# Channel attention and gated FFN on one core: the first batch's G/H tiles in other slots and PSUM banks, a bf16 epsilon product, and sums of squares folded before the norm products

## The chip, the core and the metric

The kernel runs on one core of a Trainium2 chip. The metric is the device time of one execution in microseconds (us). Five runs of the kernel before gave a median of 808.2 us (808.1 to 808.29).

## The reference

For each of 4 batches, q, k and v are 6016 x 256 matrices. Every column of q and k is divided by its norm over the 6016 rows; the 256 x 256 scores between k's and q's columns go through a softmax along the last axis; v times this matrix is the attention output. All rows then pass through a gated feed-forward layer of width 1536.

```python
B, N, C = (4, 6016, 256)
qn = q / (np.linalg.norm(q, axis=1, keepdims=True) + 1e-06)
kn = k / (np.linalg.norm(k, axis=1, keepdims=True) + 1e-06)
s = kn.transpose(0, 2, 1) @ qn / tau
s = s - s.max(-1, keepdims=True)
a = np.exp(s)
a /= a.sum(-1, keepdims=True) + 1e-09
x = (v @ a).reshape(B * S, D)
gate = 1.0 / (1.0 + np.exp(-(x @ w_gate)))
val = x @ w_val
out = gate * val @ w_out
```

## The kernel before

**G and H.** The softmax matrix and the first layer's weights are multiplied once per batch: G = a @ w_gate and H = a @ w_val, each 256 x 1536, so that v goes directly into the gated layer. A tile of G or H (`gh`) is a pair of matmuls into a PSUM tile `ps_gh` (`gh_mms`), and an eviction that divides by the row sums (`gh_store`, on ScalarE where the piece's channel block is 0, else on VectorE). For the first batch the pieces come in the order of the weight loads (`gh_first`): columns 0 to 255 and 256 to 511 (half width), then two groups of 512; in each, G's two channel blocks and then H's two. So tiles 0 to 3 serve slots 0 and 1, tiles 4 to 7 slots 2 and 3, tiles 8 to 11 slots 4 to 7, tiles 12 to 15 slots 8 to 11.

**Chunks and slots.** A batch has 47 row tiles of 128, handled in 12 chunks of 4 (the last has 3). A chunk has 12 slots, one for each 128 columns of the hidden layer. In a slot `glu` issues two matmuls into `ps_gate` and two into `ps_val` (512 columns each, both with vT, the transposed rows of v, as the moving operand), tanh on ScalarE (`g_sb`), and one VectorE operation that gives `hT`. `ps_gate` and `ps_val` have two PSUM banks each (`psg`, `psv`). So a slot's `ps_val` waits for the `hT` of two slots before.

**The second layer.** `out_work` lists the products of the chunk before with w_out, some of them with sums of blocks of `hT` that VectorE makes (`a_sum`, tile `sums`) and sums of blocks of w_out. `run_work` issues a share of them in each slot, as `ps_o`. ScalarE copies the results out, GpSimd adds blocks (`m_sb`, `out_sb`), and SyncE stores.

**Side work.** `side_work(b)` puts the preparation of batch b + 1 into the slots of batch b, counted from the batch's start (slot 98 is slot 2 of chunk 8). Loads of q, k and v are issued by GpSimd. The transposes of v (`transpose_v`) are DMA transposes issued by SyncE, one chunk ahead; only the first chunk's vT is made on TensorE. Score products go into `ps_s`. Squares of q and k (ScalarE) are added up in `acc`, a bf16 tile of 128 x 4 x 256 per tensor (`acc_add`, VectorE). Then `norms_mm` sums `acc` over partitions: for each of q and k, 4 row tiles x 2 channel blocks, a weight load of 128 x 128 and a product with one column of ones. `root_seed` (VectorE) and `root_steps` (13 small GpSimd operations) take the square root, `norms_inv` the reciprocal, `spread_both` and `copy_rk` bring k's factors into a row layout, and `exps` gives the exponentials `e_sb`.

**Row sums.** `sums_start` opens the PSUM tile `ps_r` with the product of `ones_row` and `eps_row`, one row high, which puts epsilon into it; `row_sums` adds the products of `e_sb` with ones and takes the reciprocal. For the first batch there are two such tiles, made ahead of the chunks; later batches have one each (`all_sums`, slot 116).

**The first batch's start.** Squares, scores and norms of batch 0 run ahead of the first chunk, and so do tiles 0 to 3. The other tiles are in the first chunk: tile 4 between gate and val products of slot 0 (`between` of `glu`), the rest behind the slots that `gh_slots` lists, all of them in the two banks of `pso`. The order on every engine is the order in which the program issues (`manual_schedule`).

Of the kernel before, what the change touches and what calls it, by code (L numbers as in the profile page):

```python
# [9 lines left out]
FP32 = mybir.dt.float32  # L10
BF16 = mybir.dt.bfloat16
INT32 = mybir.dt.int32
ACT = mybir.ActivationFunctionType
ALU = mybir.AluOpType
# [39 lines left out]
def kernel(  # L54
# [20 lines left out]
    nc = tc.nc  # L75
    P = nc.NUM_PARTITIONS
# [8 lines left out]
    CB = C // P  # L85
# [3 lines left out]
    TPC = 4  # L89
# [12 lines left out]
    def pool(name, bufs, **kw):  # L102
        return ctx.enter_context(tc.tile_pool(name=name, bufs=bufs, **kw))

    consts = pool("consts", 1)
# [14 lines left out]
    pso = pool("pso", 2, space=PSUM)  # L120
    pss = pool("pss", 1, space=PSUM)
    psm = pool("psm", 1, space=PSUM)
# [3 lines left out]
    def mm(out, lhsT, rhs, start, stop, **kw):  # L126
        nc.tensor.matmul(out, lhsT=lhsT, rhs=rhs, start=start, stop=stop, **kw)  # L127
# [43 lines left out]
    one_two = consts.tile([P, 2], BF16)  # L171
    nc.vector.memset(one_two[:, 0:1], 1.0)
    nc.vector.memset(one_two[:, 1:2], 2.0)
    ones_row = consts.tile([1, P], FP32)
    nc.vector.memset(ones_row, 1.0)
    eps_row = consts.tile([1, CB, 2], FP32)
    nc.vector.memset(eps_row[:, :, 0:1], 1e-9)
    nc.vector.memset(eps_row[:, :, 1:2], 2e-9)
    shift = consts.tile([P, 1], FP32)
# [12 lines left out]
    for f0, nf in pieces:  # L192
        for w, src in enumerate((moe_w_gate, moe_w_val)):
            nc.gpsimd.dma_start(
                out=w_sb[w][f0 // FG][:, :, ds(f0 % FG, nf)],
# [7 lines left out]
    for n in range(FC // TPC):  # L203
        w_f32[n] = f32pool.tile([P, TPC, C], FP32, tag="f32", name="w_f32")
        nc.gpsimd.dma_start(
            out=w_f32[n], in_=moe_w_out.rearrange("(t p) c -> p t c", p=P)[:, n * TPC : (n + 1) * TPC, :]
# [16 lines left out]
    st = {}  # L223
# [29 lines left out]
    def norm_mms(ps, sqs, nt, first, last, order=(0, 1)):  # L253

        for w in order:
            sq = sqs[w]
            for u in range(nt):
                for j in range(CB):
                    mm(
                        ps[:, w * CB + j : w * CB + j + 1],  # L260
                        sq[:, u, ds(j * P, P)],
                        ones_bf[:, 0:1],
                        start=(first and w == order[0] and u == 0 and j == 0),
                        stop=(last and u == nt - 1),
                        skip_group_check=True,
                    )
# [12 lines left out]
    def acc_add(b, g, w):  # L279
# [5 lines left out]
            out=acc[:, :nt, :], in0=acc[:, :nt, :], in1=st[b]["sq", w][:, :nt, :], op=ALU.add  # L285
        )

    def norms_mm(b):
        s = st[b]
        s["n"] = psm.tile([P, 2 * CB], FP32, tag="m", name="ps_n")  # L290
        norm_mms(s["n"], s["acc"], TPC, True, True)

    def scale_x(b, j):
        s = st[b]
# [143 lines left out]
    gh_first = [(f0, nf, w, i) for f0, nf in pieces for w in range(2) for i in range(CB)]  # L438
# [15 lines left out]
    def gh_store(b, piece, ps, act):  # L454
        s = st[b]
        f0, nf, w, i = piece
        dst = s["gh"][w][f0 // FG][:, i, ds(f0 % FG, nf)]
        if act:
            nc.scalar.activation(out=dst, in_=ps[:, :nf], func=ACT.Copy, scale=s["rrow"][i][w])
        else:  # L460
            nc.vector.tensor_scalar(  # L461
                out=dst, in0=ps[:, :nf], scalar1=s["rrow"][i][w], scalar2=None, op0=ALU.mult
            )

    def gh(b, piece, pl, tag, act=None):
        gh_store(b, piece, gh_mms(b, piece, pl, tag), piece[3] == 0 if act is None else act)
# [25 lines left out]
    def glu(b, ci, f, between=None):  # L492
        t0, nt = groups[ci]
        n = nt * P
        G, H = st[b]["gh"]
        vT = vts[b, ci]
        if f == 0:
            hts[b, ci] = hpool.tile([P, FC, CH], BF16, tag="hT", name="hT")
        ps_gate = psg.tile([P, CH], FP32, tag="g", name="ps_gate")
        ps_val = psv.tile([P, CH], FP32, tag="v", name="ps_val")  # L500
        for ps, w in ((ps_gate, G), (ps_val, H)):
            for ib in range(CB):
                mm(
                    ps[:, :n],
                    w[f // (FG // P)][:, ib, ds(f % (FG // P) * P, P)],
                    vT[:, ib, :nt, :],
                    start=(ib == 0),
                    stop=(ib == CB - 1),
                )
            if between is not None and w is G:  # L510
                between()
        g_sb = gpool.tile([P, CH], FP32, tag="g", name="g_sb")
        nc.scalar.activation(out=g_sb[:, :n], in_=ps_gate[:, :n], func=ACT.Tanh, scale=0.5)  # L513
        nc.vector.scalar_tensor_tensor(  # L514
            out=hts[b, ci][:, f, :n],
            in0=g_sb[:, :n],
            scalar=1.0,
            in1=ps_val[:, :n],
            op0=ALU.add,
            op1=ALU.mult,  # L520
        )
# [123 lines left out]
    def store():  # L645
        while stores:
            b, ci = stores.pop(0)
            t0, nt = groups[ci]
            nc.sync.dma_start(out=out_rows[b][:, t0 : t0 + nt, :], in_=ffn.pop((b, ci))[:, :nt, :])
# [40 lines left out]
    acc = st[0]["acc"]  # L690
    last0 = len(groups0) - 1
    adds, ends = [], []
    for g, (t0, nt) in enumerate(groups0):
# [6 lines left out]
        while adds:  # L700
            w, last_sq = adds.pop()
# [42 lines left out]
    def side_work(b):  # L744


        side = {}

        def at(slot, fn, *a):
            side.setdefault(divmod(slot, FC), []).append((fn, a))  # L750

        for ci in range(NCH):
            nb, nci = (b, ci + 1) if ci + 1 < NCH else (b + 1, 0)
            lb, lci = (b, ci + 2) if ci + 2 < NCH else (b + 1, ci + 2 - NCH)
            if nb < B:
                at(ci * FC + 2, transpose_v, nb, nci)
            if lb < B:
                at(ci * FC + 0, load_v, lb, lci)
            if (b, ci) == (0, 0):
                for i in range(FC // TPC):  # L760
                    at(8, copy_w_out, i)
                for n, m in enumerate((1, 0, 3, 2, 4)):
                    for i in range(FC // TPC):
                        at(10 + 2 * n, sum_w_out, m, i)
        n = b + 1
        if n == B:
            return side
        first, last = (14 if b == 0 else 0), 8 * FC
        for g, (t0, nt) in enumerate(groups):
            s0 = first + g * (last - first) // NCH  # L770
            if b == 0:
                at(max(0, s0 - 12), load_qk, n, t0, nt)
            elif s0 >= 24:
                at(s0 - 24, load_qk, n, t0, nt)
            for u in range(nt):
                at(first + (t0 + u) * (last - first) // NT, score, n, t0, u)
            if g == 0:
                at(s0, acc_start, n)
            for i, (fn, w) in enumerate(((acc_square, 0), (acc_add, 0), (acc_square, 1), (acc_add, 1))):
                at(s0 + 1 + 2 * i, fn, n, g, w)  # L780
        if n + 1 < B:
            for g, (t0, nt) in enumerate(groups[:3]):
                at(NCH * FC - 24 + 8 * g, load_qk, n + 1, t0, nt)
        s0 = 8 * FC + 2
        at(s0, norms_mm, n)
        at(s0 + 1, root_seed, n)
        at(s0 + 1, root_steps, n)
        at(s0 + 10, norms_inv, n)
        at(s0 + 12, spread_both, n)
        at(s0 + 13, copy_rk, n)  # L790
        at(s0 + 14, scale_x, n, 0)
        at(s0 + 14, scale_x, n, 1)
        at(s0 + 15, exps, n, 0)
        at(s0 + 16, exps, n, 1)
        at(s0 + 18, all_sums, n)
        at(s0 + 18, gh_tiles, n)
        for i, piece in enumerate(gh_order):
            at(s0 + 19 + 9 * i // 4, gh, n, piece, *((pss, "s"), (psm, "m"))[i % 2])
        return side

    gh_slots = ((5, 6, 7), (8,), (9, 10), (11,), (12,), (13, 14), (15,))
    prev = None
    for b in range(B):
        side = side_work(b)
        for ci in range(NCH):
            final = (b, ci) == (B - 1, NCH - 1)
            for f in range(FC):
                first = (b, ci, f) == (0, 0, 0)  # L810
                glu(b, ci, f, (lambda: gh(0, gh_first[4], pso, "o")) if first else None)
                if prev is not None:
                    if f == 4:
                        store()
                    if f + final in NEXT_SLOTS and prev != (0, 0):
                        a_sum(*prev, 1, NEXT_SLOTS[f + final])
                    run_work(work, 1 / max(1, FC - final - f))
                if f in OWN_SLOTS and not final and (b, ci) != (0, 0):
                    a_sum(b, ci, 0, OWN_SLOTS[f])
                for fn, a in side.get((ci, f), ()):  # L820
                    fn(*a)
                if (b, ci) == (0, 0) and f < len(gh_slots):
                    for i in gh_slots[f]:
                        gh(0, gh_first[i], pso, "o")
            prev = (b, ci)
            if not final:
                work = out_work(*prev)
# [39 lines left out]
```

## Time and profile before

| | |
|---|---|
| median of 5 runs | 808.2 us (808.1 to 808.29) |
| the profiled execution | 808.1 us |
| its span | 806.3 us |
| TensorE busy | 786.7 us, 98% of the span |
| VectorE busy | 704.3 us, 87% |
| ScalarE busy | 525.6 us, 65% |
| GpSimd busy | 356.8 us, 44% |
| share of TensorE in the chain that ended last | 94% |

The profile is one execution recorded by the hardware. PE is TensorE's matmuls, PEld its weight loads (they overlap), DVE VectorE, ACT ScalarE, POOL GpSimd, SP SyncE; an engine name with a q is its queue of DMA issues. A row of a timeline has the start in us, the length in us, engine, line, operation and tiles (output <- inputs), how many operations were merged, and in brackets the idle time before it and what ended that. A row of the waits has the total in us, the number of waits, and the longest. A row of the groups ends with busy us, mean ns of one, and idle us before. Line 127 is the helper that issues every matmul, so matmuls are told apart by their tiles. Matmuls are pipelined: their recorded lengths overlap, and what one costs is read from the distance of starts.

### The profile page before, as it was taken

The numbers are of one execution on the slowest core, as the hardware profiler recorded it, in microseconds if no ns is written. First come the engines' busy times: TensorE is split into PE (matmuls) and PEld (weight loads), VectorE is DVE, ScalarE is ACT, GpSimd is POOL, SyncE is SP. The second block draws the span as 40 slices with busy tenths as digits, with TensorE's granted clock in tenths as the row PEclk, the third lists the DMA queues.
The fourth block names the chain that finished last, engine by engine and source line by source line (L and its number), as shares of the span: only waits on it lengthen the run. The fifth ranks groups of instructions, "written<-read, shape, count | busy, mean of one in ns | idle before, by whom it ended". The sixth has DMA issues, their size and how long they took to land.

```text
span 806.3 us, 17906 instructions
## 1 busy us (share of the span) xinstructions
PE 786.7 (98%) x6769; PEld 502.2 (62%) x6786; DVE 704.3 (87%) x1201; ACT 525.6 (65%) x890; POOL 356.8 (44%) x568
## 2 busy tenths in 40 slices
PE   4899999999999999999999999999999999999998
PEld 2546666666666666666666666666666666666666
DVE  5767999998878999999887999999988898898896
ACT  3666777766667776775666767776666665665664
POOL 4572545444452444335443544433534244434433
PEclk9999999999999999999999999999999999999999
DMA  9996757532567557422367476523322332332402
GB/s 214 204 213 107 123 92 136 103 67 47 103 125 125 90 103 146 86 53 59 82 118 132 72 145 111 106 54 89 64 53 54 86 66 63 83 66 68 85 28 74
DMA packets 78919, 78.50 MB, mean 97 GB/s; under 512 B 51824, under 2 KB 56688, under 8 KB 78832
## 3 DMA queue, kind: packets, MB, share of 16 engines
q0 software_dynamic: 22192, 39.59, 30.0%
q1 hardware_dynamic: 56064, 36.91, 20.2%
q8 instruction: 53, 0.87, 0.5%
q10 hardware_dynamic: 576, 0.85, 0.3%
q14 instruction: 34, 0.28, 0.1%
HBM read 78.64 MB, written 24.64 MB: 128 GB/s over the span
## 4 chain that ended last, share of the span: by engine, by line
PE 94%; DMA 3%; DVE 1%; issue 1%; POOL 0%; ACT 0%; POOLq 0%; DVEq 0%; ACTq 0%
PE ps_val L127 30%; PE ps_gate L127 30%; PE ps_o L127 27%; PE ps_s L127 4%; DMA k_sb<-in_k_dram 3%; PE ps_gh L127 2%; DVE hT L514 0%; PE ps_r L127 0%; PE ps_n L127 0%; DVE acc L284 0%; DVE sums L536 0%; PE ps_rk L127 0%; POOL q_sb L137 0%; PE ps_end L127 0%; ACT g_sb L513 0%
## 5 line engine op out<-in xcount | busy, mean ns | idle before, releaser
L513 ACT ACTIVATE g_sb<-ps_gate 128x512 f32<-128x512 f32 (+1 forms) x576 | 338.2, 588 | 225.5 <-PE ps_gate L127 218.3
L514 DVE SCALAR_TENSOR_TENSOR hT<-g_sb,ps_val 128x512 bf16<-128x512 f32 (+1 forms) x576 | 384.5, 670 | 84.4 <-ACT g_sb L513 74.6
L127 PE MATMUL ps_val<-vT,gh_H 128*128 128x512 bf16 (+1 forms) x1152 | 337.7, 375 | 0.9 <-DVE gh_H L461 0.6
L127 PE MATMUL ps_gate<-vT,gh_G 128*128 128x512 bf16 (+1 forms) x1152 | 337.7, 375 | 0.0
L536 DVE TENSOR_TENSOR sums<-hT 128x768 bf16<-128x768 bf16 (+1 forms) x460 | 275.9, 600 | 0.0
L127 PEld LDWEIGHTS <-sums 128*128 128x128 bf16 x2670 | 183.0, 98 | 82.1
L127 PEld LDWEIGHTS <-gh_H 128*128 128x128 bf16 x1152 | 112.6, 98 | 132.4 <-DVE gh_H L461 1.4
L607 POOL TENSOR_TENSOR out_sb<-out_sb,m_sb 128x256 f32<-128x256 f32 x89 | 78.6, 884 | 239.7 <-ACT out_sb L597 211.1
L127 PE MATMUL ps_o<-w_sums,sums 128*128 128x128 bf16 x1602 | 154.4, 219 | 0.0
L127 PEld LDWEIGHTS <-hT 128*128 128x128 bf16 x1200 | 88.3, 98 | 46.9
L591 POOL TENSOR_TENSOR m_sb<-m_sb 128x128 f32<-128x128 f32 x89 | 42.2, 474 | 159.9 <-ACT m_sb L590 159.9
L127 PEld LDWEIGHTS <-gh_G 128*128 128x128 bf16 x1152 | 97.0, 98 | 14.9 <-DVE gh_G L461 0.3
L127 PE MATMUL ps_o<-w_out_sb,sums 128*128 128x128 bf16 x1068 | 96.2, 219 | 0.0
L127 PE MATMUL ps_o<-w_sums,hT 128*128 128x128 bf16 x1068 | 95.5, 219 | 0.0
L127 PE MATMUL ps_s<-k_sb,q_sb 128*128 128x256 bf16 x376 | 70.8, 292 | 13.8 <-DMA k_sb<-in_k_dram 6.9
L608 POOL TENSOR_TENSOR out_sb<-out_sb 128x256 f32<-128x256 f32 x89 | 76.9, 865 | 7.0
L597 ACT COPY out_sb<-ps_o 128x512 f32<-128x512 f32 x89 | 52.1, 586 | 12.0 <-PE ps_o L127 9.2
L284 DVE TENSOR_TENSOR acc<-acc,sq 128x1024 bf16<-128x1024 bf16 (+1 forms) x66 | 59.7, 905 | 0.0
L592 POOL TENSOR_TENSOR m_sb<-m_sb 128x128 f32<-128x128 f32 x89 | 53.8, 604 | 7.0
L246 ACT ACTIVATE sq<-k_sb 128x1024 bf16<-128x1024 bf16 (+2 forms) x44 | 44.8, 1027 | 12.0 <-DMA k_sb<-in_k_dram 12.0
L127 PEld LDWEIGHTS <-q_sb 128*128 128x128 bf16 x376 | 33.7, 104 | 19.8 <-issue 9.4
L590 ACT COPY m_sb<-ps_o 128x384 f32<-128x384 f32 x89 | 42.6, 478 | 3.4 <-PE ps_o L127 0.6
(83 smaller groups left out, 305.6 us busy)
## 6 DMA issues: line engine op xcount, KB each, us to landing
out_dram<-out_sb SPq DMA_DIRECT2D x43, 512.0 KB, 3.4
v_sb<-in_v_dram POOLq DMA_DIRECT2D x44, 256.0 KB, 5.3
q_sb<-in_q_dram POOLq DMA_DIRECT2D x35, 256.0 KB, 4.6
k_sb<-in_k_dram POOLq DMA_DIRECT2D x35, 256.0 KB, 7.3
q_sb<-in_q_dram POOLq DMA_DIRECT2D x4, 512.0 KB, 11.5
k_sb<-in_k_dram POOLq DMA_DIRECT2D x4, 512.0 KB, 13.4
w_f<-in_moe_w_out_dram POOLq DMA_DIRECT2D x3, 512.0 KB, 9.3
out_dram<-out_sb SPq DMA_DIRECT2D x3, 384.0 KB, 2.8
```

The costliest lines, as they stand in the source:

```text
L127: nc.tensor.matmul(out, lhsT=lhsT, rhs=rhs, start=start, stop=stop, **kw)
L246: nc.scalar.activation(out=sq[:, :nt, :], in_=src[:, :nt, :], func=ACT.Square)
L284: nc.vector.tensor_tensor(out=acc[:, :nt, :], in0=acc[:, :nt, :], in1=st[b]["sq", w][:, :nt, :], op=ALU.add)
L513: nc.scalar.activation(out=g_sb[:, :n], in_=ps_gate[:, :n], func=ACT.Tanh, scale=0.5)
L514: nc.vector.scalar_tensor_tensor(out=hts[b, ci][:, f, :n], in0=g_sb[:, :n], scalar=1.0, in1=ps_val[:, :n], op0=ALU.add, op1=ALU.mult,)
L536: nc.vector.tensor_tensor(out=sums[b, ci, g][:, m, :, : half * P], in0=hT[:, f0 + k0 : f1 : 2, ds(r0 * half * P, half * P)], in1=hT[:, f0 ...
L590: nc.scalar.copy(m, states[p]["ps"][:, : 3 * P].rearrange("p (n c) -> p n c", c=P))
L591: nc.gpsimd.tensor_tensor(out=m[:, 1, :], in0=m[:, 1, :], in1=m[:, 2, :], op=ALU.add)
L592: nc.gpsimd.tensor_tensor(out=m[:, 2, :], in0=m[:, 1, :], in1=m[:, 0, :], op=ALU.add)
L597: nc.scalar.copy(o[:, p : p + half + 1 : half, :], states[p]["ps"].rearrange("p (t c) -> p t c", c=C),)
L607: add(out=ends, in0=ends, in1=states[p]["m"][:, 1:3, :], op=ALU.add)
L608: add(out=ends, in0=ends, in1=mids, op=ALU.subtract)
```

## The change

It has three parts.

1. In the first chunk, tiles 4, 6, 9 and 11 are issued between the gate and val products of slots 0 to 3, and the other tiles one or two at the ends of slots 0 to 6. Tiles take their PSUM tiles in rotation from `pso`, `psm`, `pso` and `pss` (`gh_banks`), four banks where there were two.
2. `ones_row` and `eps_row` are bf16 where they were FP32. The compiled product is one weight load and one matmul; before it was an FP32 product that runs as two passes.
3. For batches 1 to 3, a new `acc_fold` adds the four row tiles of `acc` to one on VectorE (128 x 512, then 128 x 256 elements, for each of q and k), and `norms_mm` uses that one row tile: 4 products where there were 16. The folds are at slots 98 and 99 in batch 0 and at 96 and 98 in batches 1 and 2; `norms_mm` moves from slot 98 to 101, `root_seed` and `root_steps` from 99 to 102. `norms_inv` stays at 108. In GpSimd's queue the root steps now stand behind one more pair of `m_sb` adds.

```diff
-    ones_row = consts.tile([1, P], FP32)
+    ones_row = consts.tile([1, P], BF16)
     nc.vector.memset(ones_row, 1.0)
-    eps_row = consts.tile([1, CB, 2], FP32)
+    eps_row = consts.tile([1, CB, 2], BF16)
...
+    def acc_fold(b, w):
+        acc = st[b]["acc"][w]
+        for n in (2, 1):
+            nc.vector.tensor_tensor(out=acc[:, :n, :], in0=acc[:, :n, :], in1=acc[:, n : 2 * n, :], op=ALU.add)
+
     def norms_mm(b):
         s = st[b]
         s["n"] = psm.tile([P, 2 * CB], FP32, tag="m", name="ps_n")
-        norm_mms(s["n"], s["acc"], TPC, True, True)
+        norm_mms(s["n"], s["acc"], 1, True, True)
...
         s0 = 8 * FC + 2
-        at(s0, norms_mm, n)
-        at(s0 + 1, root_seed, n)
-        at(s0 + 1, root_steps, n)
+        at(s0 if b == 0 else s0 - 2, acc_fold, n, 0)
+        at(s0 + 1 if b == 0 else s0, acc_fold, n, 1)
+        at(s0 + 3, norms_mm, n)
+        at(s0 + 4, root_seed, n)
+        at(s0 + 4, root_steps, n)
         at(s0 + 10, norms_inv, n)
...
-    gh_slots = ((5, 6, 7), (8,), (9, 10), (11,), (12,), (13, 14), (15,))
+    gh_mid = {0: 4, 1: 6, 2: 9, 3: 11}
+    gh_end = {0: (5,), 1: (7, 8), 2: (10,), 3: (12,), 4: (13,), 5: (14,), 6: (15,)}
+    gh_banks = ((pso, "o"), (psm, "m"), (pso, "o"), (pss, "s"))
+
+    def gh_piece(n):
+        gh(0, gh_first[n], *gh_banks[n % 4])
+
     prev = None
...
             for f in range(FC):
-                first = (b, ci, f) == (0, 0, 0)
-                glu(b, ci, f, (lambda: gh(0, gh_first[4], pso, "o")) if first else None)
+                mid = gh_mid.get(f) if (b, ci) == (0, 0) else None
+                glu(b, ci, f, None if mid is None else (lambda: gh_piece(mid)))
...
-                if (b, ci) == (0, 0) and f < len(gh_slots):
-                    for i in gh_slots[f]:
-                        gh(0, gh_first[i], pso, "o")
+                if (b, ci) == (0, 0):
+                    for i in gh_end.get(f, ()):
+                        gh_piece(i)
```

## The prediction

> **What bounds the kernel now.** I read the page first (busy time, chain), then TensorE's waits, then the three stretches the change touches.
>
> ```profile
> PE 786.7 (98%) x6769; PEld 502.2 (62%) x6786; DVE 704.3 (87%) x1201; ACT 525.6 (65%) x890; POOL 356.8 (44%) x568
> PE 94%; DMA 3%; DVE 1%; issue 1%; POOL 0%; ACT 0%; POOLq 0%; DVEq 0%; ACTq 0%
> ```
>
> TensorE is 98% busy and 94% of the chain, VectorE second at 87%. TensorE's waits from 36 us to the end:
>
> ```profile
> PE ps_val L127 <- DVE gh_H L461: 0.6, 1, 0.6
> PE ps_gh L127 <- ACT gh_H L459: 0.6, 1, 0.6
> PE ps_val L127 <- DVE hT L514: 0.3, 1, 0.3
> ```
>
> Only 1.5 us in all. So the change can pay in two ways: it takes instructions out of TensorE's stream, or it removes G/H waits in the first chunk. The timeline of that chunk (start, length, engine):
>
> ```profile
> 36.70 0.73 PE L127 MATMUL ps_gate<-vT,gh_G 128*128 128x512 bf16 x2
> ...
> 39.16 0.38 PE L127 MATMUL ps_gh<-w_val,e_sb 128*128 128x256 bf16 x2 [0.56 <-ACT gh_H L459]
> ...
> 43.37 19.88 SPq L478 DMA_TRANSPOSE vT<-v_sb  x3
> ...
> 45.21 0.39 PE L127 MATMUL ps_val<-vT,gh_H 128*128 128x512 bf16 x1 [0.64 <-DVE gh_H L461]
> ...
> 53.28 0.59 PE L127 MATMUL ps_gate<-vT,gh_G 128*128 128x512 bf16 x2
> ```
>
> Slot 0 of the first chunk begins at 36.70, the next chunk at 53.28. In between stand the two G/H waits, and the first DMA transpose, which makes the next chunk's vT.
>
> **Part 1, G/H tiles.** TensorE's work between these times: neighbouring pairs of 512 columns start 0.432 us apart (52.41, 52.85, 53.28), of 256 columns 0.22. Twelve slots of two pairs are 10.37, tiles 4 to 7 (half width) 0.86, tiles 8 to 15 3.46: 14.69. The stretch takes 16.58, so 1.89 is waiting. Of this 0.13 is slot 0's gate product waiting for the first G tile, which the change leaves. At stake: 1.76.
>
> I walked the new order through with the durations of these rows (eviction of 512 columns: 0.69 on ScalarE, 0.74 on VectorE, beginning 0.41 after a pair's second matmul starts; tanh 0.60; hT 0.69; every engine in order). With four banks in rotation no tile waits for a bank; the tightest point is slot 8, where tile 15 is stored at 48.67 and its reader would start at 48.72 (a wait of 0.02). The same walk over the old order ends 0.26 later than the trace does, so it errs to the slow side. The weights are there: they land (issue plus time to landing) at 38.3, 39.5, 40.8 and 42.1, and their first readers now start at 39.4, 41.2, 42.9 and 45.5. So TensorE would reach the next chunk at 51.54.
>
> What is late next is vT. Its transpose was issued at 43.37, as soon as v_sb had landed (issue 34.84 + 8.5 = 43.34), and takes
>
> ```profile
> vT<-v_sb SPq DMA_TRANSPOSE x1, 9.4
> ```
>
> to landing: 52.77. Before, that lay 0.5 us ahead of its reader and was no wait. No load in front of it waits for TensorE's progress (GpSimd's loads there wait for earlier loads), so it does not move. TensorE will wait from 51.54 to about 52.83: the gain is 53.28 - 52.83 = **0.45** of the 1.76. Bounds: 0.3 if the landing slips as little as 0.15, 1.74 if it did not hold TensorE.
>
> That new idle of 1.3 us is near what the clock bears:
>
> ```profile
> 19.03:22.45 3.42, 2.04 (x18) 1.76 (x17) 2.39 (x5) 1.91 (x2) 1.06 (x2) 1.00 1.08 216
> 22.45:25.86 3.41, 1.30 (x7) 0.53 (x6) 3.06 (x5) 0.54 (x2) 0.53 (x1) 1.00 1.06 208
> 25.86:29.27 3.41, 3.41 (x16) 2.22 (x14) 2.73 (x5) 3.41 (x5) 1.77 (x3) 0.50 1.12 209
> ```
>
> (window, length, PE busy; the third number from the end is the granted clock.) A stretch with 1.30 us busy was followed by one at half clock, a stretch with 2.04 busy was not. The new one has at least 2.1 busy: I cost it at nothing. A dip would cost 3.41/2 = 1.7 us.
>
> **Part 2, norms of batches 1 to 3.** Slot 98 of batch 0:
>
> ```profile
> 173.77 0.54 PE L127 MATMUL ps_n<-ones_bf,acc 128*128 128x1 bf16 x16
> ...
> 174.07 0.67 DVE L514 SCALAR_TENSOR_TENSOR hT<-g_sb,ps_val 128x512 bf16<-128x512 f32 x1
> 174.17 0.59 PE L127 MATMUL ps_gate<-vT,gh_G 128*128 128x512 bf16 x2
> ...
> 175.43 0.69 DVE L514 SCALAR_TENSOR_TENSOR hT<-g_sb,ps_val 128x512 bf16<-128x512 f32 x1 [0.69 <-ACT g_sb L513]
> ```
>
> A slot's gate products start 1.255 us after those of the slot before; here 174.17 - 172.51 = 1.66. So 16 loads with their one-column products cost 0.405, or 25.3 ns each, all on the path. Four stay: 12 x 25.3 ns x 3 batches = **0.91** gained.
> The Trainium skill (TensorE: Matmul & The Clock Gate, section LDWEIGHTS) prices a weight load by its columns, 128 / 1.2 = 107 ns; by it this part would be an estimated 3.85 us and the time near 803.6, but the 25.3 ns are measured here, and I keep to them.
>
> The folds put four adds per batch on VectorE. Nearest rows, L248 with two bf16 inputs:
>
> ```profile
> L248 DVE TENSOR_TENSOR sq<-q_sb 128x512 bf16<-128x512 bf16 x1 | 0.4, 425 | 0.1
> L248 DVE TENSOR_TENSOR sq<-k_sb 128x256 bf16<-128x256 bf16 x1 | 0.3, 292 | 0.2 <-DMA k_sb<-in_k_dram 0.2
> ```
>
> One fold is 425 + 292 = 0.72, two are 1.43 per batch. Queued behind them are hT operations, and TensorE's ps_val needs the bank that hT frees two slots later. An hT on time ends 1.93 after its slot's gate product and its bank is wanted at 2 x 1.255 + 0.43 = 2.94: VectorE may lag 1.0 us. Batch 0: hT of slot 98 starts at 174.07, so fold 0 ends at 175.43; hT of slot 99 then is 0.3 late, sums 0.85, fold 1 until about 177.5, hT of slot 100 until 178.07, wanted at 178.07. norms_mm, now at the end of slot 101, is reached at about 177.53 and needs fold 1, done at 177.48. Both just meet: about 0.1 lost. Batches 1 and 2 fold in slots 96 and 98, which have no sums; hT of slot 96 starts at 366.01, 0.85 late, and the same addition leaves margins of 0.1 to 0.3. GpSimd adds can stretch such operations: L284 with 1024 columns has a mean of 914 ns against 691 for L704. I take **-0.15** in all, from +0.1 (fold 0 partly fills an idle that norms_mm made) to -0.9.
>
> The seed and the root steps move three slots, past one pair of m_sb adds in GpSimd's queue. From seed to result the steps took 177.0 to 181.94, about 5 us; from slot 102 to norms_inv in slot 108 there are 6 x 1.255 = 7.5. Hidden, with over 1 us left; the out_sb adds behind the steps come some 2 us later, cover the next store, due a chunk later, and cost nothing.
>
> **Part 3, epsilon product.** Batches 1 to 3:
>
> ```profile
> 197.07 0.33 PE L127 MATMUL ps_o<-w_out_sb,sums 128*128 128x128 bf16 x3
> 197.34 0.38 PE L127 MATMUL ps_r<-eps_row,ones_row 1*128 1x4 f32 x2
> 197.65 0.25 PE L127 MATMUL ps_r<-one_two,e_sb 128*128 128x2 bf16 x4
> ```
>
> From the end of ps_o's issue (197.07 + 3 x 0.056 = 197.24) to 197.65 it takes 0.41 in two passes. Full-height FP32 passes (ps_rk, 189.22 to 189.72, four of them) cost 0.126 each and leave no gap, so about 0.16 belongs to the one-row shape, which stays. No row has a one-row bf16 product; between a norm pair (0.025) and an FP32 pass (0.126) it saves 0.41 - 0.16 - (0.025 to 0.126) = 0.12 to 0.22, and 0.38 if the gap goes too. I take 0.17, the middle: 3 x 0.17 = **0.51** (0.36 to 1.14).
> The Trainium skill (same page, section Weight-path perf modes) makes a load fast when its weights are 128 columns and not FP32; by it the new pass sits at the 0.025 end, an estimated 0.66 for the three.
> In batch 0 the product lies ahead of a wait for e_sb (35.58): nothing.
>
> **Sum.** 0.45 + 0.91 + 0.51 - 0.15 = 1.72. The profiled run took 808.1 us (span 806.3 and 1.8 around it): 806.4. Against the median of 808.2: **806.5**.
>
> **Rivals.** (a) The transpose does not hold TensorE: 1.29 more, 805.2. For it, no wait for vT stands in the trace; against it, its landing lies only 0.5 ahead of the reader. 8%.
> (b) The folds just miss their margins, 0.3 a batch: -0.9 in place of -0.15, 807.3. For it, VectorE has no idle in slots 96 to 98; against it, it idles 0.7 to 1.0 us right after. 17%.
> (c) Slower: VectorE becomes the bound in slots 96 to 107. Then both folds stand on TensorE's path, 3 x 1.43 = 4.3 against 1.87 gained: 810.6. It decides once hT is 1.0 us late before the first fold; now it is 0.29 to 0.85. 10%.
> My forecast has 65%; its own range is 805.8 to 807.2 (1.0 to 2.4 gained), and somewhat over half of it lies beyond 0.2% (806.6), about what a measurement of this kernel tells from no change. Faster: 0.08 + 0.38 = 0.46; same: 0.27 + 0.17 = 0.44; slower 0.10. The range 805.2 to 808.0 leaves out (c) and the outer edges.
>
> **What would show it.** TensorE waits about 1.3 us for the vT transpose before the second chunk, and the G/H waits are gone; norm stretches of 0.1 us; epsilon stretches near 0.24; no wait for hT or acc over 0.2 in slots 98 to 104. A second chunk that starts at 51.6, a half-clock stretch after 53, or waits for hT in each batch would prove me wrong.

## The result, and the profile after

The kernel after takes 806.3 us (median of 24 runs, 806.11 to 806.63) where the kernel before takes 808.17 (44 runs, 807.97 to 808.45): a ratio of 0.9977 [0.9972, 0.9983], or 0.23% less. The forecast was 806.5. The profiled execution took 806.3 us with a span of 804.5; before it was 808.1 and 806.3.

The page of the kernel after, its busy line and its chain by engine:

```profile
PE 784.6 (98%) x6728; PEld 499.9 (62%) x6745; DVE 706.9 (88%) x1213; ACT 525.5 (65%) x890; POOL 355.1 (44%) x568
...
PE 92%; DMA 5%; POOL 1%; DVE 1%; issue 1%; POOLq 0%
```

TensorE has 41 matmuls fewer (36 norm products, in place of which VectorE has 12 adds more, and 5 second passes of epsilon products, two of them ahead of the first chunk), and 2.1 us less to do. The chain has gone from 3% to 5% DMA: what that is shows in TensorE's waits from 36 us to the end:

```profile
PE ps_gate L127 <- DMA vT<-v_sb: 1.0, 1, 1.0
PE ps_val L127 <- DVE hT L519: 0.3, 1, 0.3
```

Both G/H waits are gone, a wait for the transposed v has come in their place, and the 0.3 for hT is the one that stood there before. The timeline of TensorE in the first chunk:

```profile
36.77 0.72 PE L127 MATMUL ps_gate<-vT,gh_G 128*128 128x512 bf16 x2
...
40.79 0.78 PE L127 MATMUL ps_val<-vT,gh_H 128*128 128x512 bf16 x2
...
51.35 0.59 PE L127 MATMUL ps_val<-vT,gh_H 128*128 128x512 bf16 x2
52.97 0.60 PE L127 MATMUL ps_gate<-vT,gh_G 128*128 128x512 bf16 x2 [1.02 <-DMA vT<-v_sb]
```

The first chunk's last pair starts at 51.35; a pair takes 0.43, so TensorE is ready for the next chunk at 51.78 and gets it at 52.97. Before it was 53.28: 0.31 gained of the 1.50 that lie between 53.28 and 51.78.

The timeline of all engines about slot 101 of batch 0, with the second fold, the hT behind it, the norm products with their weight loads, and the val pair of slot 102 that needs this hT:

```profile
176.11 1.00 DVE L291 TENSOR_TENSOR acc<-acc 128x512 bf16<-128x512 bf16 x2
...
177.03 0.68 DVE L519 SCALAR_TENSOR_TENSOR hT<-g_sb,ps_val 128x512 bf16<-128x512 f32 x1
...
177.18 0.20 PEld L127 LDWEIGHTS <-acc 128*128 128x128 bf16 x4
177.23 0.24 PE L127 MATMUL ps_n<-ones_bf,acc 128*128 128x1 bf16 x4
...
177.77 0.59 PE L127 MATMUL ps_val<-vT,gh_H 128*128 128x512 bf16 x2
```

The slot with the norm products has 1.36 us from gate pair to gate pair (175.98 to 177.34), against 1.66 before; batches 1 and 2 show 1.36 too (369.39 to 370.75, 562.81 to 564.17). That is 0.30 three times, 0.90. The hT ends at 177.71, its reader starts at 177.77: the folds cost TensorE nothing, with 0.06 us to spare.

TensorE's timeline at the epsilon product of batch 1, which runs in batch 0's slots:

```profile
196.48 0.33 PE L127 MATMUL ps_o<-w_out_sb,sums 128*128 128x128 bf16 x3
196.74 0.17 PE L127 MATMUL ps_r<-eps_row,ones_row 1*128 1x4 bf16 x1
196.85 0.25 PE L127 MATMUL ps_r<-one_two,e_sb 128*128 128x2 bf16 x4
```

The issue of ps_o ends at 196.48 + 3 x 0.056 = 196.65; e_sb's products start at 196.85, 0.20 later. Before it was 0.41. The whole slot went from 1.77 to 1.57, in all three batches: 0.60. So 0.31 + 0.90 + 0.60 = 1.81, which is the 1.8 by which the span fell.

### The profile page after: what moved, and what is told of

Its sections match the earlier page's. It is cut to its first block, busy times and chain, and to the rows that moved or that the text cites. A ratio compares the mean times of both kernels' runs of the same rounds, so it can differ in the third digit from the quotient of the medians.

```text
span 804.5 us, 17835 instructions
## 1 busy us (share of the span) xinstructions
PE 784.6 (98%) x6728; PEld 499.9 (62%) x6745; DVE 706.9 (88%) x1213; ACT 525.5 (65%) x890; POOL 355.1 (44%) x568
## 4 chain that ended last, share of the span: by engine, by line
PE 92%; DMA 5%; POOL 1%; DVE 1%; issue 1%; POOLq 0%
PE ps_val L127 29%; PE ps_gate L127 29%; PE ps_o L127 27%; PE ps_s L127 4%; DMA k_sb<-in_k_dram 3%; PE ps_gh L127 2%; DMA vT<-v_sb 1%; DMA v_sb<-in_v_dram 1%; DVE hT L519 0%; POOL w_gate L194 0%; POOL w_val L194 0%; DVE acc L284 0%; DVE sums L541 0%; PE ps_rk L127 0%; PE ps_end L127 0%
```

## The experiments

All ratios are against the kernel before, whose median was 808.1 in each of these comparisons. "After" is the changed kernel.

**Each part alone.** Three kernels, each the kernel before with one part of the change.

Part 1, the G/H tiles:

```diff
-    gh_slots = ((5, 6, 7), (8,), (9, 10), (11,), (12,), (13, 14), (15,))
+    gh_mid = {0: 4, 1: 6, 2: 9, 3: 11}
+    gh_end = {0: (5,), 1: (7, 8), 2: (10,), 3: (12,), 4: (13,), 5: (14,), 6: (15,)}
+    gh_banks = ((pso, "o"), (psm, "m"), (pso, "o"), (pss, "s"))
...
```

> The kernel before with part 1 alone (slots and four banks for the G/H tiles of the first batch). Theory: the second chunk's gate product starts when vT(0,1) lands, about 52.9, so 0.3 to 0.45 us are gained: 807.8; TensorE shows a wait for vT of 1 us and none for gh_H. Rival: the rotation is worth its full 1.7 us and the wait for vT is only where the trace shows it, with something else made up later: 806.5. Second rival: the idle in front of the second chunk costs clock, and the time stays at 808.2 or goes above.

Part 2 of the prediction, the folds and the norm products:

```diff
...
-        norm_mms(s["n"], s["acc"], TPC, True, True)
+        norm_mms(s["n"], s["acc"], 1, True, True)
...
+        at(s0 if b == 0 else s0 - 2, acc_fold, n, 0)
+        at(s0 + 1 if b == 0 else s0, acc_fold, n, 1)
...
```

> The kernel before with part 3 alone (folds, four norm products per batch, later slots). Theory: 36 pairs of 25.3 ns leave TensorE's path and the folds lie in VectorE's slack: -0.9 us, 807.3; the norm slot takes 1.36 us where it took 1.66. Rival: the folds make hT late, TensorE waits about 0.3 us per batch for it: 808.1 or no change. Rival that they become the bound: 3 x 1.43 - 0.9 = 3.4 us more, 811.6.

Part 3, the epsilon product:

```diff
-    ones_row = consts.tile([1, P], FP32)
+    ones_row = consts.tile([1, P], BF16)
...
-    eps_row = consts.tile([1, CB, 2], FP32)
+    eps_row = consts.tile([1, CB, 2], BF16)
```

> The kernel before with part 2 alone (bf16 epsilon product). Theory: each of the three products on the path costs 0.20 us less, 0.6 in all: 807.6; the product in the first batch is ahead of a wait for e_sb and gives nothing. Rival: only the pass itself leaves, 0.13 us each: 807.8.

| kernel | median us (range) | ratio | span of the profiled run |
|---|---|---|---|
| G/H tiles alone | 807.9 (807.76 to 808.11) | 0.9997 [0.9988, 1.0006] | 806.0 |
| norms and folds alone | 807.41 (807.11 to 808.37) | 0.9993 [0.9984, 1.0002] | 805.5 |
| epsilon alone | 807.55 (807.36 to 807.74) | 0.9993 [0.9984, 1.0002] | 805.6 |
| all three | 806.3 (806.11 to 806.63) | 0.9977 [0.9972, 0.9983] | 804.5 |

No part alone can be told from no change by its interval. The spans tell more. Their medians over all runs are 806.1, 805.5 and 805.8, against 806.4 for the kernel before and 804.5 for all three parts: 0.3, 0.9 and 0.6, together 1.8 of the 1.9 that the whole takes off. The spans of the last two (at most 805.6 and 805.9) lie wholly below those of the kernel before (806.2 to 806.7); those of the G/H tiles alone (806.0 to 806.3) overlap them. So the parts add up, to 0.1 us. With the G/H tiles alone the wait for vT is there already (1.1 us, next chunk at 52.96), so it is made by part 1. With the folds alone TensorE has the three waits of before and no new one.

**What sets the landing of vT?** In after the transpose is issued at 43.50 and lands 9.4 us later. The prediction had this as issue time plus a duration. First test: issue it earlier. The second chunk's v is loaded ahead of the last two weight pieces, so that its transpose can start sooner.

```diff
     for f0, nf in pieces:
+        if f0 == 2 * FG:
+            load_v(0, 1)
...
-    load_v(0, 1)
```

> The changed kernel with the load of the second chunk's v issued ahead of the last two weight loads (512 KB) instead of behind them; nothing else moves. Theory: vT(0,1) is what holds the second chunk. v lands 1.2 to 1.5 us earlier (about 42.1), the transpose starts then and lands 9.4 us later at about 51.5, and TensorE's wait for vT (1.2 us between starts) goes: 805.1 to 805.4. The last G and H weights land about 0.7 to 1.3 us later (42 and 43.3) ahead of their readers at 43.1 and 45.7. Rival: the transpose's landing is set by the DMA engines' load around 45 to 52, not by its issue, and stays at 52.9: 806.3. Second rival: the weights come late, a wait for them of up to 1 us takes the place of the one removed: 806.3.

806.54 (806.23 to 808.83), ratio 0.9983 [0.9974, 0.9991]: not below after's 806.3. From the DMA issues of this kernel (number of issues, us from issue to landing), and then TensorE's waits:

```profile
vT<-v_sb SPq DMA_TRANSPOSE x1, 12.0
```

```profile
PE ps_gate L127 <- DMA vT<-v_sb: 1.1, 1, 1.1
```

The transpose was issued at 40.87, 2.63 us earlier, and took 2.6 us longer: it landed at 52.87 and TensorE went on at 52.89. The theory missed; its rival, that other loads on the DMA engines set the landing, had the time.

Second test: leave the issue where it is and take a load out from beside it. In after, GpSimd issues the load of the third chunk's v (256 KB) at 38.80, ahead of the transpose's issue; here it waits until slot 9.

```diff
-                at(ci * FC + 0, load_v, lb, lci)
+                at(9 if (b, ci) == (0, 0) else ci * FC + 0, load_v, lb, lci)
```

> The changed kernel with the load of the third chunk's v (256 KB, issued at 38.8 us and not used before 69) issued 11 us later, behind the w_out casts in GpSimd's queue. The run with the earlier v load showed that a transpose issued 2.6 us sooner still lands at 52.9, so theory: its landing is set by the loads that share the DMA engines until about 51. With 256 KB less in front, at about 205 GB/s, vT(0,1) lands 1.2 us earlier, and TensorE's wait for it all but goes: 805.1 to 805.4. Rival: the transposes wait for something else (their own issue or a fixed order behind w_out's loads), the landing stays near 52.9 and the time at 806.3.

805.02 (804.92 to 805.26), ratio 0.9962 [0.9949, 0.9974], span 803.5. The transpose, issued at 43.39, lands 8.0 us later; the wait for vT is gone, and the next chunk starts at 51.93. Why the transpose takes 1.4 us less shows in the DMA queues from 49 to 50 us (packets, MB, share of 16 engines; q0 carries GpSimd's loads, q1 the transposes and stores). After:

```profile
q0 software_dynamic: 101, 0.19, 98.4%
q1 hardware_dynamic: 99, 0.03, 18.4%
```

With the later load:

```profile
q1 hardware_dynamic: 461, 0.12, 129.5%
q0 software_dynamic: 20, 0.03, 16.4%
```

While loads are queued, the transpose gets about one packet for each of theirs, some 100 per us, and needs 1056. When few are left it gets 493 in a us (after, 50 to 51 us, beside 59 packets of loads), or 461 and 414 (later load, 49 to 51), though not steadily: from 51 to 52 after shows 245, beside 8 packets of loads. So in these two runs the landing moved with the end of the backlog, and the 256 KB taken out of it are worth, at the 0.19 MB per us of q0 here, an estimated 1.4 us, as much as the transpose took less.

The earlier transpose of the first test took its turns with the loads too, packet for packet (98, 96, 97 and 102 packets beside 97, 92, 100 and 100 of the loads in the four us from 46). But it had a head start. Its packets from 45 to 50 us (row of q1), and then those of after's transpose in the same time:

```profile
q1 hardware_dynamic: 464, 0.12, 15.7%
```

```profile
q1 hardware_dynamic: 218, 0.06, 8.2%
```

This was worth nothing, and turns with the loads alone do not say why: at 51.5 us the earlier transpose had 998 of its packets through and after's 792, yet the last 58 took until past 52. What held them is not shown.
The Trainium skill (DMA: Bandwidth & Descriptors, section Queues, rings and completion order) says that each DMA engine takes turns between the queues that have work, a packet at a time; the nearly equal counts agree, if the profile's packets are the page's.

Control: the same later load in the kernel before, where vT was no wait.

> The kernel before with nothing but the later load of the third chunk's v. Theory: in the kernel before vT(0,1) was not a wait, TensorE reached it 0.5 us after its landing, so a landing 1.2 us earlier changes nothing: 808.1. Rival: the load also slowed other things in the first chunk (w_out's loads, the first q and k tiles), and its delay alone brings part of the 1.3 us: 807 to 807.6.

808.08 (807.94 to 808.38), ratio 0.9999 [0.9991, 1.0008]. The later load brings 1.28 us to the kernel after and nothing to the kernel before: it does nothing but take away the wait that part 1 made.

The other way round the wait is to make this vT on TensorE, as the first chunk's is, from the same v_sb:

```diff
+    def first_vt():
+        ps = psm.tile([P, TPC * CB, P], BF16, tag="m", name="ps_tp")
+        transpose_v(0, 1, ps, lambda dst, src: nc.scalar.copy(dst, src))
...
-            if nb < B:
+            if (b, ci) == (0, 0):
+                at(7, first_vt)
+            elif nb < B:
```

> The changed kernel with the second chunk's vT made by 8 TensorE transposes behind slot 7 of the first chunk (as the first chunk's is), copied out by VectorE (three quarters) and ScalarE. Theory: the wait for vT (1.2 us between starts) goes for 8 x 0.056 = 0.45 us of TensorE: 0.7 less, 805.6, and no wait for vT in the trace. Rival: what was behind the wait holds it next (the w_out casts, which end at about 49, or the first q and k tiles of batch 1), and the time stays at 806.3 or above; or the copies make hT late in slots 8 to 11.

805.9 (805.57 to 807.09), ratio 0.9975 [0.9966, 0.9984]. The wait is gone and the next chunk starts at 52.17, 0.8 sooner than in after, with the eight transposes paid for in TensorE's time. The spans show the gain: 803.7 to 803.8 in nine of the eleven runs, 0.7 below after's median span of 804.5. The medians of the times lie only 0.4 apart because the time outside the span, 1.8 us in after's profiled run, is up to 3.0 in runs of this kernel. The profiled run (806.62, span 804.8) is one of the two with a long span: its last store is issued 0.8 us sooner than after's (801.02 against 801.82), but takes 2.7 us to land where after's takes 1.5. Why is not shown.

**The two halves of part 1.** With vT out of the way, what are the slots worth, and what the four banks? Both kernels have the later load. One puts all tiles back into the two banks of pso, in the new slots:

```diff
-    gh_banks = ((pso, "o"), (psm, "m"), (pso, "o"), (pss, "s"))
+    gh_banks = ((pso, "o"),) * 4
```

> The changed kernel with the later v load, but with the G/H tiles in the two banks of pso as before; only the new slots are left of part 1. Walk with the trace's durations, as in the prediction: one wait of about 0.4 us at tile 8 for its bank, the next chunk reached at 51.95 against 51.54; so 0.4 more than the run with the later load (805.0): 805.4. Rival: the banks are what matters, and the waits of the old kernel (1.76 us) come back for the most part: 806.5.

The other keeps four banks and the slots of before:

```diff
-    gh_mid = {0: 4, 1: 6, 2: 9, 3: 11}
-    gh_end = {0: (5,), 1: (7, 8), 2: (10,), 3: (12,), 4: (13,), 5: (14,), 6: (15,)}
+    gh_mid = {0: 4}
+    gh_end = dict(enumerate(((5, 6, 7), (8,), (9, 10), (11,), (12,), (13, 14), (15,))))
```

> The changed kernel with the later v load, but with the G/H tiles in the old slots; only the four banks are left of part 1. Walk with the trace's durations: the wait for a bank goes, the wait of slot 4's val product for the H tile issued just ahead of it stays (0.6 in the old trace, 0.9 in the walk), the next chunk is reached at 52.4; so 0.7 to 0.9 more than the run with the later load: 805.8. Rival: four banks are all it takes, no wait: 805.0.

Two banks: 805.78 (805.65 to 805.83), 0.9971 [0.9959, 0.9982]. Old slots: 805.74 (805.6 to 806.03), 0.9971 [0.996, 0.9982]. Their waits, besides the 0.3 for hT; two banks first:

```profile
PE ps_gh L127 <- ACT gh_G L464: 0.3, 1, 0.3
```

```profile
PE ps_val L127 <- DVE gh_H L466: 0.7, 1, 0.7
```

Each brings back the wait that its half removed: a tile that waits for its bank, and a val pair that waits for its H tile. Either way the first chunk takes 15.73 us; with both halves it was 15.02, in the kernel before 16.58. The medians stand 0.76 and 0.72 above the 805.02 with both. With two banks that is more than the 0.4 expected, and the wait row shows only 0.34 of the 0.71. The timeline has the rest: three G/H tiles, not one, start late, at 39.48, 39.78 and 41.15, by 0.30, 0.08 and 0.51 us, each 0.05 or 0.06 after a store that empties a bank has ended (39.42, 39.73, 41.10). That is 0.89, against 0.18 that the run with four banks loses in the same slots. So each half is worth some 0.7 once vT is in time; in the kernel after, vT hides most of it.

**The gap of the one-row product.** The prediction put 0.16 us of the epsilon product down to its one-row shape. Here it is full height, with epsilon / 128 in every row (and `ones_bf`, 128 x 128, in place of `ones_row`):

```diff
...
-    eps_row = consts.tile([1, CB, 2], BF16)
...
+    eps_row = consts.tile([P, CB, 2], BF16)
+    nc.vector.memset(eps_row[:, :, 0:1], 1e-9 / P)
...
-        mm(ps_r, ones_row, eps_row[:, :ni, :], start=True, stop=False, skip_group_check=True)
+        mm(ps_r, ones_bf, eps_row[:, :ni, :], start=True, stop=False, skip_group_check=True)
```

> The changed kernel with the epsilon product at full height: 128 rows of ones times 128 rows that each hold epsilon / 128, in place of one row. Theory: the 0.2 us that the product still takes is the one-row shape's gap before and after it, and a full-height bf16 product sits in the stream like the norm products, 0.03 us: 3 x 0.17 = 0.5 less than the changed kernel, 805.8. Rival: the gap belongs to the product's place (it opens a PSUM tile that other matmuls wrote before), and stays: 806.3.

805.63 (805.49 to 805.69), ratio 0.9969 [0.9956, 0.9981], span 803.8. TensorE's timeline:

```profile
196.51 0.17 PE L127 MATMUL ps_r<-eps_row,ones_bf 128*128 128x4 bf16 x1
196.54 0.24 PE L127 MATMUL ps_r<-one_two,e_sb 128*128 128x2 bf16 x4
```

The same product at full height costs 0.03 us from start to start, where ps_o's end to e_sb's first product was 0.20 with one row. Three times 0.17 is 0.51; 0.67 was measured against after's median. In the profiled runs 0.14 of that lies ahead of the second chunk already (it starts at 52.83 and not at 52.97), where the start differs from run to run; why the medians differ by as much is not shown.
The Trainium skill (TensorEngine Tiling (Array Packing), section Key Properties) says that a change of tiling mode drains TensorE. That would fit a product of one row among products of 128; no run here shows the drain itself.

**The slack of VectorE.** The hT with 0.06 us to spare says that the folds just fit. Two more adds of the size of the first one, behind the second fold of each batch, into a tile that nobody reads:

```diff
+        if w == 1:
+            for _ in range(2):
+                idle = attp.tile([P, 2, C], BF16, tag="idle", name="idle")
+                nc.vector.tensor_tensor(out=idle, in0=acc[:, 2:4, :], in1=acc[:, 2:4, :], op=ALU.add)
```

> The changed kernel with two more VectorE adds of 128x512 (0.43 us each) behind the second fold of each batch, into a tile that nobody reads. Theory: VectorE's margin in slots 98 to 104 is all but used up. In the trace of the changed kernel hT of slot 100 ends 0.06 us ahead of its reader in batch 0, and hT of slot 99 some 0.35 us ahead in batches 1 and 2; so 0.86 us more give waits for hT of about 0.8, 0.55 and 0.55 us: 808.2. Rival: the PSUM banks and the slots without sums absorb most of it, and the time rises by less than 0.5 us: 806.3 to 806.8.

808.95 (808.73 to 809.11), ratio 1.0009 [1.0001, 1.0018], span 807.2. TensorE's waits:

```profile
PE ps_val L127 <- DVE hT L523: 2.4, 4, 0.7
PE ps_gate L127 <- DMA vT<-v_sb: 1.2, 1, 1.2
```

The added adds took a mean of 556 ns, 1.1 us per batch, and cost 2.65 in all, 0.88 per batch. The theory had 1.9, with 430 ns for an add. In batch 0 the two took 0.88 and cost 0.79 (the val pair of slot 102 starts 1.22 after its gate pair, at 178.60, where it is 0.43 in after). In batches 1 and 2, where GpSimd adds `m_sb` at the same time, they took 1.28 and cost 0.89. So VectorE has 0.1 us of slack left here in batch 0 and 0.4 in the other two, and rival (c), which makes the change a loss, is two adds away: this kernel is slower than the one before.

**Both repairs together**, the later load and the full-height epsilon:

> The changed kernel with both the later load of the third chunk's v and the epsilon product at full height. Theory: the two lie in different stretches (the first chunk; slot 116 of batches 0 to 2) and add up: 806.3 - 1.25 - 0.65 = 804.4. Rival: with the wait for vT gone, something else in the first two chunks moves when batch 0's two epsilon products do, and less than the sum comes: 804.9.

804.49 (804.39 to 804.82), ratio 0.9955 [0.9943, 0.9968], span 802.7: the fastest here, 1.8 us below after. TensorE has one wait left, the 0.3 for hT.

## Why the prediction was right

The total was right (806.5 against 806.3), and no term was off by more than 0.15. Some of that is luck: the first term was 0.14 too high, the folds and the epsilon product together 0.24 too low, and these partly cancel.

| term | predicted | measured |
|---|---|---|
| G/H tiles | 0.45 | 0.31 |
| norm products | 0.91 | 0.90 |
| folds | -0.15 | 0 |
| epsilon product | 0.51 | 0.60 |
| sum | 1.72 | 1.81 |

**Norm products.** 25.3 ns each was right: the four that are left take 0.105, 26 ns each. The Trainium skill (TensorE: Matmul & The Clock Gate, section LDWEIGHTS) gives 107 ns for a load of 128 columns by its rule; the trace records a load of acc as 94 to 98 ns long, but the loads overlap (the four together take 0.20), so this is not what one costs here.

**Folds.** The prediction let hT of slot 100 end just when it was wanted, both at 178.07. It ended at 177.71 and was wanted at 177.77 (the run being 0.3 ahead of the one before by then), although the second fold took 1.00 us and not 0.72, beside an add of m_sb on GpSimd. So the -0.15 was not spent, but the extra adds show that it was near. Rival (b) had the right place and was just missed. GpSimd's root steps took 4.57 us in batch 1 and delayed nobody.

**Epsilon.** The mechanism was right in both halves: one pass goes and the one-row gap stays. The size was 0.20 a batch where the middle of 0.12 to 0.22 gave 0.17. The gap that stays, 0.17 by the full-height run, is the 0.16 that the prediction worked out with the rows of ps_rk.

**G/H tiles.** That vT takes over as the wait was right, and so was its consequence: of about 1.5 us freed, 0.31 is kept. The term is 0.14 off, since v landed so that the transpose was issued at 43.50 and not at 43.37: 0.13, which goes directly into the term. Other kernels here that load this v as after does issue it between 43.20 and 43.57, so this looks like scatter and not the change. The walk that had TensorE ready at 51.54 was 0.24 off, and vT covered that: the chunk starts 0.07 later (36.77), and the walk missed a wait in slot 2. A weight load in that slot, from the timeline of all engines:

```profile
41.17 0.10 PEld L127 LDWEIGHTS <-gh_H 128*128 128x128 bf16 x1 [0.50 <-DVE gh_H L466]
```

Tile 7's store on VectorE stands behind the hT of slot 1, ends at 41.12, and the val pair's second matmul needs it. It costs 0.19; without the vT wait the chunk takes 15.02, where the walk had 51.54 - 36.70 = 14.84. So the walk did not err to the slow side, as its check on the old order had suggested.

One step gave the right number by a wrong reason. "No load in front of it waits for TensorE's progress, so it does not move" looked at what stands ahead of the issue. The landing is not issue plus 9.4: it was 12.0 with an earlier issue and 8.0 with one load less beside it. That 9.4 held fits the loads beside it, which the change left where they were. The later load makes rival (a)'s case, a vT that does not hold TensorE: 805.02 where the rival had 805.2.

**Clock.** The stretch with the wait was costed at nothing. The windows of after (length, PE busy, then the other engines; granted clock third from the end):

```profile
49.75:53.16 3.41, 2.39 (x12) 0.90 (x10) 2.57 (x4) 1.79 (x3) 3.40 (x6) 1.00 1.23 182
```

2.39 us are busy here, and the next stretch (53.10 to 56.51) is at clock 1.00: no dip.

## What to carry to other kernels

A freed wait is worth the distance to the next-latest arrival, so work out what that is before counting the gain; here 1.5 us were freed and 0.31 kept, until one load of 256 KB was moved out of the way for another 1.28. When a DMA is the next arrival, ask what shares the DMA engines while it runs, not only when it is issued: here issuing earlier into a backlog gained nothing, taking a load out of the backlog did. Try a small product at the full height of its neighbours (0.17 us each here), and before work is moved to an engine off the path, work out its slack at that place: VectorE was idle 12% of the span and had 0.1 us at the tightest of the three places.

## What the runs showed of the hardware that was not expected

- A DMA transpose of 1056 packets issued 2.63 us earlier landed at the same time (52.87 against 52.9). Beside queued loads the transposes moved about 100 packets per us, and up to 414 to 493 when few loads were left.
- A one-row product among full-height ones costs 0.20 us in bf16 and the same product at full height 0.03; the 0.17 between them is the shape's.
- An add of 128 x 512 on VectorE took a mean of 456 ns in the folds and 556 ns in the run with two more of them. Beside GpSimd's adds of m_sb two of the added ones took 1.28 us (batches 1 and 2), in batch 0, where one ran beside only their last 0.2 us, 0.88; the second fold of batch 0 took 1.00 with such an add beside 0.4 us of it, the other folds 0.74 with at most 0.15. No run changes this alone.
